# Sparse attention and two expert layers on one core: zero rows beside the last keys, and a new way through the fourth step

## The chip, the cores and the metric

The kernel runs on one core of one Trainium2 chip. The metric is the device time of one execution in microseconds, as a median over runs. TensorE does the matmuls, VectorE (DVE) and ScalarE (ACT) the element-wise work, GpSimd (POOL) part of it, and SyncE (SP) issues the DMAs.

## The reference

The reference chains three layers. Attention has 2 batches, 8 heads, 576 tokens and a head size of 64; each row of scores keeps its 32 largest entries. Its output, 1152 x 512, goes through four experts (512 to 1024 to 512, ReLU), weighted by shares per token, and then through a gated layer (512 to 1536 to 512).

```python
scores = scale * np.matmul(q, k.transpose(0, 1, 3, 2))
kth = np.partition(scores, -top_k, axis=-1)[..., -top_k:-top_k + 1]
scores = np.where(scores >= kth, scores, -1000000000.0)
scores = scores - np.max(scores, axis=-1, keepdims=True)
attn = np.exp(scores)
attn = attn / (np.sum(attn, axis=-1, keepdims=True) + 1e-09)
x = np.matmul(attn, v)                       # then 1152 x 512
for e in range(E):
    out += p[:, e:e + 1] * (np.maximum(x @ w1[e], 0.0) @ w2[e])
return ((out @ w_a) * (out @ w_b)) @ w_out
```

## The kernel before

The 1152 tokens are nine tiles of 128 rows: four per batch for its first 512 tokens, and one mixed tile (MIX) with the last 64 tokens of both batches. The tiles are split into groups of 1, 2, 3 and 3 (SIZES). Attention runs in 36 steps, numbered n, from 0: for each group, for each of four pairs of heads, for each tile of the group. Steps 0 to 3 are the first group, 4 to 11 the second, 12 to 23 the third, 24 to 35 the fourth; the four mixed steps lie in the last.

A step does the same for both heads of the pair, called x. TensorE makes 128 x 576 scores (`scores`), and ScalarE copies them into a score place (`ss`, four places). `masked` finds the 32 largest on VectorE: four times MAX8 (line 603) with three MATCH_REPLACE8 between them (609), into a weight place (`es`, six places). Then GpSimd multiplies the largest and the 32nd value by constants (649), ScalarE makes Relu with a very steep slope, zero for what is kept (656), GpSimd subtracts it (659), ScalarE takes exp with the sum beside it (666), GpSimd adds 1e-9 (675), VectorE takes the reciprocal (676), and ScalarE scales (679). In step 3, called URGENT, each head goes through this chain alone, and the difference and the addition stand on VectorE (659, 673). `weigh` turns the weights on TensorE, copies them out of PSUM (706, 710) into one of three places `pt`, and multiplies them with v: four blocks of 128 keys and one of the last 64 (`vrem`), for each head in one half of TensorE's columns. At the end of a pair its result goes into `xf` (738, first group) or `xs` (744, 746, the others), as the input of the experts.

The first group's experts (`plain`) work in plain float32; the others (`experts`) and the gated layer split each value into a high and a low part. A weight unit of 512 KB lands in one of three places `raw`, or, for every fourth unit of `plain`, in `pw`; for `experts` ScalarE (767) and GpSimd or VectorE (768) split it.

The order of the work is not that of the code. Each piece is an Op with an engine, an estimated hold, a lag until others see it, a due time (`key`) and its inputs and buffers; `Plan.order` walks through the estimated time and always takes the ready piece with the smallest key. What comes out is a fixed list for each engine, and each engine works through its own in order: an instruction whose input isn't there holds all those behind it. Keys of attention are near n; those of expert matmuls begin at 1000 and of weight loads at 500, so that they fill what attention leaves.

Of the kernel before, what the change touches and what calls it, by code (L numbers as in the profile page):

```python
# [16 lines left out]
TOPK = 32  # L17
# [220 lines left out]
PAIRED, URGENT = (), 3  # L238


def body(tc, q, k, v, probs, w1, w2, wa, wb, wo, out):
# [42 lines left out]
    ident = const("ident", [128, 128])  # L284
    identr = const("identr", [128, 128], F32R)
    pr = const("pr", [128, NT, E])
# [5 lines left out]
    vrem = [const(f"vrem{b}", [REM, H, D]) for b in range(B)]  # L292
# [91 lines left out]
    def consts():  # L384
        make_identity(nc, ident)
        nc.vector.tensor_copy(identr, ident)
        nc.gpsimd.memset(qm.bitcast(F32), 0.0)
        nc.gpsimd.memset(facs[:, :, 0], -scale)
        nc.gpsimd.memset(facs[:, :, 1], STEEP)

    ready = gpsimd(1900, consts, -1e6, (), ())

    loads = []
    for i, t in enumerate(TILES):
        for rows_, view in token_rows(t, probs):
            loads.append(load(lambda i=i, rows_=rows_: pr[rows_, i], lambda view=view: view, 2.0, nbytes=4096))
# [7 lines left out]
    shared = vector(900, shares, 3.5, loads, ())  # L404
# [13 lines left out]
    def keys(b, h2, key, eng):  # L418
# [27 lines left out]
        for j in range(2):  # L446
# [8 lines left out]
            o = tensor(5 * TURN_R, turn, key + 0.02, sp[j] + krem_done[b][h + j] + [ready], [at, st_])  # L455
# [21 lines left out]
    def start_pair(c, h2, n):  # L477
# [65 lines left out]
        for b in batches(tiles):  # L543
            vt = vts.tile(n)
            pair.v[b] = vt
            pair.vd[b] = [load(
                lambda vt=vt: vt.ap.rearrange("p (h m d) -> p h m d", h=2, m=M4), lambda b=b: main_rows(v, b, h), n - 2.5, (), [vt]
            )]
            if b not in vrem_done:
                vrem_done[b] = load(lambda b=b: vrem[b], lambda b=b: last_rows(v, b), n - 2.4, (), (), 131072)  # L550
        return pair

    def scores(pair, j, i, n):
# [24 lines left out]
        o = tensor(4 * len(bs) * mm_r(HALF), emit, n - AHEAD, after, [at] + used)  # L578
# [8 lines left out]
    def masked(sd, n):  # L587

        m8, ends, sums = m8s.tile(), endss.tile(), sumss.tile()
        W = TOPK + 17 if n in PAIRED else TOPK  # L590
        m8v = lambda: m8.ap[:, 0:2 * W].rearrange("p (x n) -> p x n", x=2)
# [3 lines left out]
        last = []  # L595

        def top(x, src, c0, rounds, width, key, done):

            for r in range(rounds):
# [5 lines left out]
                )  # L605
                if r < rounds - 1:
# [9 lines left out]
        for x in range(2):  # L616
            s = sd[x][0]
            key = n + (0.4 if urgent else 0.001) * x
            if n not in PAIRED:
                last.append(top(x, [lambda s=s: s.ap, lambda x=x: e[x].ap], 0, TOPK // 8, S, key, sd[x][1]))  # L620
                continue


            got = []
            for i, op in enumerate((ALU.max, ALU.min)):
                half = lambda x=x, i=i: e[x].ap[:, i * HALF:(i + 1) * HALF]
                po = gpsimd(
                    pool_(HALF), lambda s=s, half=half, op=op: nc.gpsimd.scalar_tensor_tensor(half(), s.ap[:, 0:HALF], 1.0, s.ap[:, HALF:S], op0=ALU.mult, op1=op),
                    n - 0.4 + 0.1 * i, [sd[x][1]], [s, e[x]],
                )  # L630
                got.append(top(x, [half, half], TOPK * i, TOPK // 8 // (i + 1), HALF, key + 0.005 * i, po))

            o = vector(
                85, lambda x=x: nc.vector.tensor_tensor(
                    m8v()[:, x, TOPK:TOPK + 16], m8v()[:, x, TOPK - 2:TOPK - 18:-1], m8v()[:, x, TOPK:TOPK + 16], op=ALU.min
                ), -600, got, [m8],
            )
            last.append(vector(
                85, lambda x=x: nc.vector.tensor_reduce(
                    out=m8v()[:, x, TOPK + 16:W], in_=m8v()[:, x, TOPK - 1:TOPK + 16], axis=mybir.AxisListType.X, op=ALU.max  # L640
                ), -600, [o], [m8],
            ))

        ks = -3000 if urgent else n + 0.1
        out_, ex = [], []
        for xs_ in ([0], [1]) if urgent else ([0, 1],):
            x0, x1 = xs_[0], xs_[-1] + 1
            en = gpsimd(
                150, lambda x0=x0, x1=x1: nc.gpsimd.tensor_tensor(endv()[:, x0:x1], m8v()[:, x0:x1, ::W - 1], facs[:, x0:x1], op=ALU.mult),  # L649
                -4000 if urgent else -500, [last[x] for x in xs_] + [ready], [m8, ends],  # L650
            )
            for x in xs_:
                s = sd[x][0]

                a = scalar(
                    S, lambda x=x, s=s: nc.scalar.activation(e[x].ap, s.ap, AF.Relu, bias=endv()[:, x, 1:2], scale=-STEEP),  # L656
                    ks, [en], [s, e[x], ends], sbuf=True, ptr=True,
                )
                sub = lambda eng, x=x, s=s: eng.tensor_tensor(e[x].ap, s.ap, e[x].ap, op=ALU.subtract)  # L659
                if urgent:  # L660
                    b = vector(dve(S), lambda sub=sub: sub(nc.vector), ks, [a], [s, e[x]], port=True)
                else:
                    b = gpsimd(pool_(S), lambda sub=sub: sub(nc.gpsimd), ks, [a], [s, e[x]])
                ex.append(scalar(
                    S,
                    lambda x=x: nc.scalar.activation(  # L666
                        e[x].ap, e[x].ap, AF.Exp, bias=endv()[:, x, 0:1], scale=scale, accum_out=sums.ap[:, x:x + 1]
                    ),
                    ks, [b], [e[x], ends, sums], sbuf=True, ptr=True, extra=92,
                ))  # L670
            sv = lambda x0=x0, x1=x1: sums.ap[:, x0:x1]
            if urgent:
                sm = vector(70, lambda sv=sv: nc.vector.tensor_scalar(sv(), sv(), 1e-9, None, op0=ALU.add), ks, ex[-1:], [sums])
            else:
                sm = gpsimd(290, lambda sv=sv: nc.gpsimd.tensor_scalar(sv(), sv(), 1e-9, None, op0=ALU.add), -500, ex, [sums])
            rc = vector(70, lambda sv=sv: nc.vector.reciprocal(sv(), sv()), ks if urgent else -500, [sm], [sums])  # L676
            for x in xs_:
                out_.append((e[x], scalar(
                    S, lambda x=x: nc.scalar.activation(e[x].ap, e[x].ap, AF.Copy, scale=sums.ap[:, x:x + 1]),  # L679
                    ks, [rc], [e[x], sums], sbuf=True, ptr=True,  # L680
                )))
# [4 lines left out]
    def weigh(pair, i, ed, n):  # L686
# [6 lines left out]
        for e, done in ed:  # L693
# [8 lines left out]
            o = tensor(4 * TURN_F + 40, turn, n + 0.5, [done, ready], [at, e])  # L702
# [16 lines left out]
        def emit():  # L719

            for r0, r1, b in groups:
                for m in range(M4 + 1):
                    for j in range(2):
                        vt = pair.v[b].ap.rearrange("p (h m d) -> p h m d", h=2, m=M4)
                        l, rows = (vt[:, j, m], 128) if m < M4 else (vrem[b][:, pair.h + j], REM)
                        mm(
                            ov()[j * D:(j + 1) * D, i, r0:r1], l, pt[j].ap[0:rows, m * 128 + r0:m * 128 + r1],
# [4 lines left out]
            1150, emit, n + 0.6, ptd + sum((pair.vd[b] for b in bs), []) + [vrem_done[b] for b in bs], [pair.o] + pt + [pair.v[b] for b in bs]  # L732
# [44 lines left out]
    def plain_unit(src, a):  # L777
        s = nxt()
        plains[0] += 1
        r = (wraws if plains[0] % 4 else pws).tile()  # L780
# [301 lines left out]
```

## Time and profile before

| | us |
|---|---|
| median of 3 runs | 867.97 (867.55 to 869.35) |
| the profiled execution | 866.53 |
| its span, first to last instruction | 864.7 |
| TensorE busy | 826.5 |
| VectorE busy | 715.8 |
| ScalarE busy | 544.6 |
| GpSimd busy | 265.2 |

The mean granted TensorE clock was 0.998. Busy time of TensorE includes overlapping matmuls, so the start of one group of records and that of the next tell more about a group's price than its own length does. Idle time behind an engine's name in square brackets is what it stood still ahead of an instruction, with what released it.

### The profile page before, as it was taken

To read this page: it belongs to the slowest core of one execution; us is meant where nothing else is said; L and a number is where in the kernel's file an instruction comes from. 1 tells how busy PE (TensorE), PEld (TensorE's weight loads), DVE (VectorE), ACT (ScalarE), POOL (GpSimd) and SP (SyncE) were. 2 spreads that over 40 slices of the span, in tenths; PEclk is the share of its full clock that TensorE was granted. 3 is DMA by queue.
4 is the path that set the end of the run, shared out by engine and by line. 5 is a ranking of instruction groups with operands and counts; after the bars stand their busy time and mean duration, and the time that the engine had idled before them with its cause. 6 is when DMAs were issued, how large, how long until landed. Compare 5 with 4: busy or idle time off the path is not lost. (4 is left out here: it accounts for less than half of the span.)

```text
span 864.7 us, 14129 instructions
## 1 busy us (share of the span) xinstructions
PE 826.5 (96%) x5168; PEld 728.0 (84%) x5168; DVE 715.8 (83%) x1381; ACT 544.6 (63%) x1042; POOL 265.2 (31%) x245
## 2 busy tenths in 40 slices
PE   5579999999999999999999999999999999999997
PEld 4466777788888888889888888889999989999996
DVE  6899999999999999999978999555434888999723
ACT  5888987899989998877765655333324535344310
POOL 2634442887897965853320000000000000000000
PEclk9999999999999999999999999999999999999999
DMA  7727977844564444342234556434101313323003
GB/s 197 244 90 257 297 239 235 268 149 145 168 185 150 152 148 153 98 123 97 75 122 156 179 177 195 122 122 128 44 1 49 98 49 98 91 81 98 25 1 109
DMA packets 83509, 117.06 MB, mean 135 GB/s; under 512 B 10608, under 2 KB 54640, under 8 KB 83440
## 3 DMA queue, kind: packets, MB, share of 16 engines
q1 hardware_dynamic: 83440, 116.17, 42.9%
q8 instruction: 40, 0.66, 0.3%
q14 instruction: 29, 0.24, 0.1%
HBM read 109.07 MB, written 7.08 MB: 134 GB/s over the span
## 5 line engine op out<-in xcount | busy, mean ns | idle before, releaser
L603 DVE MAX8 low<-low 128x8 f32<-128x576 f32 x288 | 203.7, 747 | 3.4 <-ACT low L582 3.3
L362 PE MATMUL ps<-xs,mid 128*128 128x384 f32 (+1 forms) x1152 | 205.1, 322 | 1.3 <-POOL mid L768 1.0
L362 PE MATMUL ps<-mid 128*128 128x512 f32 x768 | 198.6, 396 | 2.1 <-DVE mid L841 2.0
L362 PEld LDWEIGHTS ps<-xs,mid 128*128 128x128 f32 x1152 | 184.4, 189 | 11.5 <-issue 2.5
L362 PEld LDWEIGHTS ps<-mid 128*128 128x128 f32 x768 | 139.2, 188 | 28.5 <-DVE mid L841 6.0
L609 DVE MATCH_REPLACE8 low<-low 128x576 f32<-128x576 f32 x216 | 159.3, 743 | 0.0
L362 PE MATMUL ps<-xs,big 128*128 128x384 f32 x864 | 152.8, 335 | 0.0
L362 PEld LDWEIGHTS ps<-xs,big 128*128 128x128 f32 x864 | 149.9, 188 | 1.6 <-DVE low L1033 0.3
L767 ACT ACTIVATE mid<-raw 128x1024 fp32r<-128x1024 f32 x96 | 101.5, 1059 | 66.3 <-issue 39.9
L768 POOL TENSOR_TENSOR mid<-raw,mid 128x1024 fp32r<-128x1024 f32 x48 | 115.2, 2408 | 11.9 <-ACT mid L767 8.9
L659 POOL TENSOR_TENSOR low<-low 128x576 f32<-128x576 f32 x70 | 98.9, 1428 | 32.8 <-ACT low L656 31.0
L362 PE MATMUL ps<-big,mid 128*128 128x512 f32 x324 | 75.1, 390 | 0.0
L768 DVE TENSOR_TENSOR mid<-raw,mid 128x1024 fp32r<-128x1024 f32 x48 | 58.5, 1220 | 18.9 <-ACT mid L767 18.7
L362 PEld LDWEIGHTS ps<-big,mid 128*128 128x128 f32 x324 | 60.7, 188 | 12.3
L837 ACT ACTIVATE mid<-ps 128x384 fp32r<-128x384 f32 (+1 forms) x96 | 42.7, 450 | 33.0 <-PE ps L362 28.3
L859 DVE SCALAR_TENSOR_TENSOR ys<-ps,pr,ys 128x512 f32<-128x512 f32 x56 | 41.5, 747 | 24.3 <-PE ps L362 23.7
L841 DVE SCALAR_TENSOR_TENSOR mid<-ps,mid 128x384 fp32r<-128x384 f32 (+1 forms) x96 | 48.0, 506 | 15.1 <-ACT mid L837 14.6
L656 ACT ACTIVATE low<-low 128x576 f32<-128x576 f32 x72 | 53.4, 772 | 7.6 <-POOL low L649 7.4
L1012 ACT ACTIVATE low<-ps 128x384 f32<-128x384 f32 x36 | 17.6, 489 | 64.1 <-PE ps L362 64.0
L365 PE MATMUL ps<-ident,low 128*128 128x128 f32 (+1 forms) x360 | 50.6, 282 | 7.3 <-ACT low L679 7.1
L679 ACT ACTIVATE low<-low 128x576 f32<-128x576 f32 x72 | 52.9, 776 | 6.1 <-DVE low L676 6.1
L666 ACT ACTIVATE low<-low 128x576 f32<-128x576 f32 x72 | 55.7, 774 | 0.7 <-POOL low L659 0.7
(76 smaller groups left out, 1040.0 us busy)
## 6 DMA issues: line engine op xcount, KB each, us to landing
raw<-in_moe_w_dram SPq DMA_DIRECT2D x120, 512.0 KB, 3.7
big<-kscr SPq DMA_DIRECT2D x20, 576.0 KB, 4.8
low<-in_v_dram SPq DMA_DIRECT2D x24, 256.0 KB, 4.1
low<-in_moe_w_a_dram SPq DMA_DIRECT2D x12, 512.0 KB, 3.8
low<-in_moe_w_b_dram SPq DMA_DIRECT2D x12, 512.0 KB, 3.8
low<-in_moe_w_out_dram SPq DMA_DIRECT2D x12, 512.0 KB, 3.6
kscr<-big SPq DMA_DIRECT2D x8, 576.0 KB, 4.4
ys<-in_moe_w_dram SPq DMA_DIRECT2D x8, 512.0 KB, 4.6
```

Source lines behind the costliest of these rows:

```text
L362: nc.tensor.matmul(out, l, r, **kw)
L365: nc.tensor.transpose(out, a, i)
L603: 62 + 1.04 * width, lambda at=at, cs=cs: nc.vector.max(m8v()[:, x, cs], at()), key + 0.02 * r, [done],
L609: lambda at=at, cs=cs: nc.vector.match_replace(out=src[1](), in_to_replace=m8v()[:, x, cs], in_values=at(), imm_value=LOW),
L656: S, lambda x=x, s=s: nc.scalar.activation(e[x].ap, s.ap, AF.Relu, bias=endv()[:, x, 1:2], scale=-STEEP),
L659: sub = lambda eng, x=x, s=s: eng.tensor_tensor(e[x].ap, s.ap, e[x].ap, op=ALU.subtract)
L666: lambda x=x: nc.scalar.activation(e[x].ap, e[x].ap, AF.Exp, bias=endv()[:, x, 0:1], scale=scale, accum_out=sums.ap[:, x:x + 1]),
L679: S, lambda x=x: nc.scalar.activation(e[x].ap, e[x].ap, AF.Copy, scale=sums.ap[:, x:x + 1]),
L767: hi = scalar(1024, lambda: nc.scalar.activation(u.ap[:, 0:1024], r.ap, AF.Copy), 500 + s, [ld], [u, r], sbuf=True)
L768: sub = lambda eng: eng.tensor_tensor(u.ap[:, 1024:2048], r.ap, u.ap[:, 0:1024], op=ALU.subtract)
L837: n, lambda h=h, p=p: nc.scalar.activation(h.ap[:, 0:n], p.ap[:, 0:n], AF.Relu), -1000, [o], [h, p]
L841: lambda h=h, p=p: nc.vector.scalar_tensor_tensor(h.ap[:, n:2 * n], p.ap[:, 0:n], 0.0, h.ap[:, 0:n], op0=ALU.max, op1=ALU.subtract),
```

## The change

- The last block of keys is multiplied over 128 rows: `vrem` and the last column block of each `pt` have zeros in rows 64 to 127, filled once by GpSimd (`zeros`, with a hold of 1500 and key 0.2). Each weighting waits for that.
- The identity for float32 turns is the same memory as the one for float32r, so 128 words are free. It is made in `xf` first.
- `raw` has four places instead of three; the attention region is 500 words smaller, all that was unused. In `plain` every fifth unit goes to `pw`.
- The lag of the GpSimd addition ahead of the reciprocal gets 1200 ns more (SLACK). That moves later in VectorE's list what the list supposes to be ready later.
- Step 3 goes through a new function `hurried`. When the first MAX8 of a head is there, GpSimd makes the bias from the largest value and ScalarE takes exp of all 576 scores into another weight place, beside the rest of the top-32. When the 32nd value is there, VectorE multiplies with (score >= 32nd) and sums, adds 1e-9, takes the reciprocal and multiplies.
- Estimates are changed: a turn of keys 640 instead of 440, scores 30 more, a turn of weights 40 more, a weighting 1245 instead of 1150. The ten loads of the shares have key 4.0 instead of 2.0, and the shares themselves 5.2 instead of 3.5.
- The branch for half-width top-32 (PAIRED, empty) is taken out. `experts` takes a unit from `ahead` where one is there; nothing puts one there.

```diff
-PAIRED, URGENT = (), 3
+SLACK = 1200
+URGENT = 3
...
-    ident = const("ident", [128, 128])
     identr = const("identr", [128, 128], F32R)
+    ident = identr.bitcast(F32)
...
-    vrem = [const(f"vrem{b}", [REM, H, D]) for b in range(B)]
+    vrem = [const(f"vrem{b}", [128, H, D]) for b in range(B)]
...
-    raw = Region("raw", 3 * 1024, F32)
-    wraws = raw.slots("wraw", 3, 1024)
-    low = Region("low", 12800, F32)
+    raw = Region("raw", 4 * 1024, F32)
+    wraws = raw.slots("wraw", 4, 1024)
+    low = Region("low", 12300, F32)
...
-        make_identity(nc, ident)
-        nc.vector.tensor_copy(identr, ident)
+        make_identity(nc, xf[:, 0])
+        nc.vector.tensor_copy(identr, xf[:, 0])
...
+    def zeros():
+        for b in range(B):
+            nc.gpsimd.memset(vrem[b][REM:128], 0.0)
+        for p in pts.aps:
+            nc.gpsimd.memset(p[REM:128, MAIN:MAIN + 128], 0.0)
+    zeroed = gpsimd(1500, zeros, 0.2, [ready], ())
...
-            loads.append(load(lambda i=i, rows_=rows_: pr[rows_, i], lambda view=view: view, 2.0, nbytes=4096))
+            loads.append(load(lambda i=i, rows_=rows_: pr[rows_, i], lambda view=view: view, 4.0, nbytes=4096))
...
-    shared = vector(900, shares, 3.5, loads, ())
+    shared = vector(900, shares, 5.2, loads, ())
...
-            o = tensor(5 * TURN_R, turn, key + 0.02, sp[j] + krem_done[b][h + j] + [ready], [at, st_])
+            o = tensor(640, turn, key + 0.02, sp[j] + krem_done[b][h + j] + [ready], [at, st_])
...
-        o = tensor(4 * len(bs) * mm_r(HALF), emit, n - AHEAD, after, [at] + used)
+        o = tensor(4 * len(bs) * mm_r(HALF) + 30, emit, n - AHEAD, after, [at] + used)
...
+                if r == 0:
+                    firsts.append(done)
...
+        if urgent:
+            return hurried(sd, n, m8v, m8, ends, endv, sums, firsts, last)
...
+        sm.lag += SLACK
+        rc = vector(70, lambda: nc.vector.reciprocal(sums.ap, sums.ap), -500, [sm], [sums])
...
+    def hurried(sd, n, m8v, m8, ends, endv, sums, firsts, last):
+        out_ = []
+        for x in range(2):
+            s, e = sd[x][0], es.tile(n)
+            en = gpsimd(
+                150, lambda x=x: nc.gpsimd.tensor_tensor(endv()[:, x, 0:1], m8v()[:, x, 0:1], facs[:, x, 0:1], op=ALU.mult),
+                -4000, [firsts[x], ready], [m8, ends],
+            )
+            ex = scalar(
+                S, lambda x=x, s=s, e=e: nc.scalar.activation(e.ap, s.ap, AF.Exp, bias=endv()[:, x, 0:1], scale=scale),
+                n + 0.1, [en], [s, e, ends], sbuf=True, ptr=True,
+            )
+            sv = lambda x=x: sums.ap[:, x:x + 1]
+            def mask(x=x, s=s, e=e, sv=sv):
+                nc.vector.scalar_tensor_tensor(
+                    e.ap, s.ap, m8v()[:, x, TOPK - 1:TOPK], e.ap, op0=ALU.is_ge, op1=ALU.mult, accum_out=sv()
+                )
+                nc.vector.tensor_scalar(sv(), sv(), 1e-9, None, op0=ALU.add)
+                nc.vector.reciprocal(sv(), sv())
+                nc.vector.tensor_scalar(e.ap, e.ap, sv(), None, op0=ALU.mult)
+            out_.append((e, vector(1450, mask, -3000, [ex, last[x]], [s, e, m8, sums], port=True)))
+        return out_
...
-            o = tensor(4 * TURN_F + 40, turn, n + 0.5, [done, ready], [at, e])
+            o = tensor(4 * TURN_F + 80, turn, n + 0.5, [done, ready], [at, e])
...
-                        l, rows = (vt[:, j, m], 128) if m < M4 else (vrem[b][:, pair.h + j], REM)
+                        l = vt[:, j, m] if m < M4 else vrem[b][:, pair.h + j]
                         mm(
-                            ov()[j * D:(j + 1) * D, i, r0:r1], l, pt[j].ap[0:rows, m * 128 + r0:m * 128 + r1],
+                            ov()[j * D:(j + 1) * D, i, r0:r1], l, pt[j].ap[:, m * 128 + r0:m * 128 + r1],
                             start=(m == 0), stop=(m == M4),
                         )
...
-            1150, emit, n + 0.6, ptd + sum((pair.vd[b] for b in bs), []) + [vrem_done[b] for b in bs], [pair.o] + pt + [pair.v[b] for b in bs]
+            1245, emit, n + 0.6, [zeroed] + ptd + sum((pair.vd[b] for b in bs), []) + [vrem_done[b] for b in bs], [pair.o] + pt + [pair.v[b] for b in bs]
...
-        r = (wraws if plains[0] % 4 else pws).tile()
+        r = (wraws if plains[0] % 5 else pws).tile()
...
-    ydone = {}
+    ydone, ahead = {}, {}
...
-                    unit = w_unit(w1[e, :, u:u + 256].rearrange("(a p) n -> p a n", p=128), KD, late)
+                    unit = ahead.pop(u) if u in ahead else w_unit(w1[e, :, u:u + 256].rearrange("(a p) n -> p a n", p=128), KD, late)
```

## Rows read from the trace of the kernel before

**Rows 1.** The page, busy us (share of the span) and instructions of each engine.
```profile
PE 826.5 (96%) x5168; PEld 728.0 (84%) x5168; DVE 715.8 (83%) x1381; ACT 544.6 (63%) x1042; POOL 265.2 (31%) x245
```
**Rows 2.** Stretches: length, busy us of PE, PEld, DVE, ACT, POOL, PE clock, DMA share, GB/s.
```profile
9.45:53.22 43.77, 28.48 (x173) 23.65 (x172) 39.26 (x83) 34.60 (x75) 21.45 (x28) 0.96 0.64 189
53.22:66.34 13.12, 10.25 (x91) 7.72 (x89) 13.02 (x33) 10.63 (x26) 3.14 (x5) 1.00 0.42 134
66.34:153.20 86.86, 84.74 (x632) 65.70 (x633) 82.91 (x179) 72.19 (x146) 35.05 (x42) 1.00 0.80 258
153.20:305.30 152.10, 148.66 (x1118) 129.41 (x1118) 148.92 (x324) 137.55 (x271) 128.83 (x95) 1.00 0.55 171
305.30:457.90 152.60, 150.96 (x1086) 133.61 (x1084) 138.82 (x275) 119.91 (x241) 75.07 (x68) 1.00 0.37 118
457.90:860.20 402.30, 398.76 (x2057) 363.89 (x2055) 289.25 (x486) 164.11 (x274) 0.00 (x0) 1.00 0.31 95
```
**Rows 3.** Timelines of DVE and PE (start, length, what): the third group's handover.
```profile
304.78 0.56 DVE L746 TENSOR_TENSOR xs<-ps,xs 128x384 fp32r<-128x384 f32 x1
...
306.52 0.69 PE L362 MATMUL ps<-xs,mid 128*128 128x384 f32 x3
```
**Rows 4.** Timeline of PE: a plain weighting with what follows, then part of a mixed one.
```profile
201.71 1.09 PE L362 MATMUL ps<-low 128*64 128x128 f32 x16
202.73 0.44 PE L362 MATMUL ps<-low,vrem 64*64 64x128 f32 x4
203.10 0.80 PE L362 MATMUL ps<-big 128*128 128x288 f32 x4
...
333.64 0.69 PE L362 MATMUL ps<-low 128*64 128x64 f32 x16
334.25 0.33 PE L362 MATMUL ps<-low,vrem 64*64 64x64 f32 x4
334.52 0.69 PE L362 MATMUL ps<-low 128*64 128x64 f32 x16
```
**Rows 5.** Groups of PE by shape: count, busy us and mean ns, idle before.
```profile
L362 PE MATMUL ps<-low,vrem 64*64 64x128 f32 x128 | 13.9, 294 | 0.0
...
L362 PE MATMUL ps<-low,vrem 64*64 64x64 f32 x32 | 2.7, 242 | 0.0
```
**Rows 6.** Timeline of DVE: the reciprocals of steps 0 to 2.
```profile
29.98 0.17 DVE L676 RECIPROCAL low<-low 128x2 f32<-128x2 f32 x1 [2.90 <-POOL low L675]
...
42.31 0.17 DVE L676 RECIPROCAL low<-low 128x2 f32<-128x2 f32 x1 [0.86 <-POOL low L675]
...
50.37 0.17 DVE L676 RECIPROCAL low<-low 128x2 f32<-128x2 f32 x1 [0.36 <-POOL low L675]
```
**Rows 7.** Timelines of DVE, ACT and PE: the end of step 3.
```profile
51.89 1.41 DVE L603 MAX8 low<-low 128x8 f32<-128x576 f32 x2
...
54.67 1.41 DVE L659 TENSOR_TENSOR low<-low 128x576 f32<-128x576 f32 x2
...
58.85 1.44 ACT L679 ACTIVATE low<-low 128x576 f32<-128x576 f32 x2
...
66.01 0.28 ACT L738 ACTIVATE xf<-ps 128x128 f32<-128x128 f32 x1 [1.82 <-PE ps L362]
...
62.90 1.67 PE L362 MATMUL ps<-big 128*128 128x288 f32 x8
```
**Rows 8.** Groups of DVE by shape: a product with one operand in the gated layer.
```profile
L971 DVE TENSOR_SCALAR low<-low 128x512 f32<-128x512 f32 x36 | 15.2, 422 | 10.3 <-ACT low L970 10.3
```
**Rows 9.** Timeline of POOL: a fill at the start, a difference of step 2.
```profile
1.23 0.95 POOL L387 MEMSET qm<- 128x1024 f32 x1
...
44.88 1.42 POOL L659 TENSOR_TENSOR low<-low 128x576 f32<-128x576 f32 x1 [0.89 <-ACT low L656]
```
**Rows 10.** Timeline of DVE: the copy of the identity and what follows.
```profile
1.32 1.01 DVE L386 CAST identr<-ident 128x128 fp32r<-128x128 f32 x1 [1.32 <-POOL ident masks.py:199]
3.99 1.36 DVE L411 TENSOR_TENSOR big<-low,big 128x256 fp32r<-128x256 f32 x5 [1.66 <-ACT big L409]
```

More of the change, by code (lines that the diff above doesn't have):

```diff
@@ L549, in start_pair @@
             if b not in vrem_done:
-                vrem_done[b] = load(lambda b=b: vrem[b], lambda b=b: last_rows(v, b), n - 2.4, (), (), 131072)
+                vrem_done[b] = load(lambda b=b: vrem[b][0:REM], lambda b=b: last_rows(v, b), n - 2.4, (), (), 131072)
         return pair
@@ L594, in masked @@
         e = [es.tile(n) for _ in range(2)]
-        last = []
+        last, firsts = [], []
         def top(x, src, c0, rounds, width, key, done):
@@ L618, in masked @@
             key = n + (0.4 if urgent else 0.001) * x
[L619 to L629, printed above, removed]
-                )
-                got.append(top(x, [half, half], TOPK * i, TOPK // 8 // (i + 1), HALF, key + 0.005 * i, po))
@@ L633, in masked @@
[L633 to L681, printed above, removed]
@@ new lines, in masked @@
+            last.append(top(x, [lambda s=s: s.ap, lambda x=x: e[x].ap], 0, TOPK // 8, S, key, sd[x][1]))
+        if urgent:
+            return hurried(sd, n, m8v, m8, ends, endv, sums, firsts, last)
+        ks = n + 0.1
+        out_, ex = [], []
+        en = gpsimd(
+            150, lambda: nc.gpsimd.tensor_tensor(endv(), m8v()[:, :, ::TOPK - 1], facs, op=ALU.mult), -500, last + [ready], [m8, ends]
+        )
+        for x in range(2):
+            s = sd[x][0]
+            a = scalar(
+                S, lambda x=x, s=s: nc.scalar.activation(e[x].ap, s.ap, AF.Relu, bias=endv()[:, x, 1:2], scale=-STEEP),
+                ks, [en], [s, e[x], ends], sbuf=True, ptr=True,
+            )
+            b = gpsimd(
+                pool_(S), lambda x=x, s=s: nc.gpsimd.tensor_tensor(e[x].ap, s.ap, e[x].ap, op=ALU.subtract), ks, [a], [s, e[x]]
+            )
+            ex.append(scalar(
+                S,
+                lambda x=x: nc.scalar.activation(
+                    e[x].ap, e[x].ap, AF.Exp, bias=endv()[:, x, 0:1], scale=scale, accum_out=sums.ap[:, x:x + 1]
+                ),
+                ks, [b], [e[x], ends, sums], sbuf=True, ptr=True, extra=92,
+            ))
@@ new lines, in masked @@
+        sm = gpsimd(290, lambda: nc.gpsimd.tensor_scalar(sums.ap, sums.ap, 1e-9, None, op0=ALU.add), -500, ex, [sums])
+        sm.lag += SLACK
+        rc = vector(70, lambda: nc.vector.reciprocal(sums.ap, sums.ap), -500, [sm], [sums])
+        for x in range(2):
+            out_.append((e[x], scalar(
+                S, lambda x=x: nc.scalar.activation(e[x].ap, e[x].ap, AF.Copy, scale=sums.ap[:, x:x + 1]),
+                ks, [rc], [e[x], sums], sbuf=True, ptr=True,
+            )))
+        return out_
```

14 lines of the change are left out of this document (9 added, 5 removed).

## The prediction

> **What bounds the kernel now.** I read the busy shares first, then the engines stretch by stretch, then single waits. TensorE is busy 826.5 of 864.7 us [rows 1], so the first idea is that only its own work counts. The stretches show otherwise [rows 2]. From 9.45 to 66.34 us TensorE is busy 38.7 of 56.9 us, while VectorE is busy 39.26 of 43.77 and then 13.02 of 13.12: here the top-32 loops of steps 0 to 3 set the pace, and each us that VectorE stands still delays the first expert stage. From 66.34 on TensorE has 2.12 + 3.44 + 1.64 + 3.54 = 10.7 us idle in 794 us and sets the end. But up to 305.30 VectorE is nearly full too (82.91 of 86.86, 148.92 of 152.10): it is a second bound there, and after 305.30 it is not.
>
> How far apart the two are shows where the third group is handed over to the experts: VectorE writes the last part of the third group's input at 304.78 to 305.34, and TensorE takes it at 306.52 [rows 3]. So TensorE has 1.2 us in hand there. A gain of TensorE alone ahead of 305 is worth that much and what other work it can pull forward; the rest has to come from VectorE.
>
> **The change, part by part.**
>
> *Zero rows.* A plain step's weighting has 16 records of 128 rows in 1.02 us and 4 of 64 rows in 0.37 us [rows 4]. Records come in pairs, one for each half of the columns. With s for a pair and E for what each change of the array's shape adds, 8s + E = 1.02 and 2s + E = 0.37, so s = 0.108 and E = 0.154 us. In a step that mixes both batches 8s + E = 0.61 and 2s + E = 0.27 [rows 4]: s = 0.057, E = 0.156, and there are four such blocks. With 128 rows throughout a plain step has one block instead of two (one E less), a mixed step one instead of four (0.47 less). The 64-row records number 128 and 32 [rows 5]: 32 plain and 4 mixed steps. Four plain steps lie ahead of 66.34, where TensorE waits anyway: nothing. 20 lie between 66.34 and 305.30: 3.1 us. The last 8 plain and the 4 mixed: 1.23 + 1.87 = 3.1 us. Sum 6.2 us, at the least 5 (if the longer block has a slower end than its pieces). The added rows cost no time of their own: a matmul's price here goes by its columns, and these stay.
>
> *Later reciprocals.* Three reciprocals stand at the head of VectorE's queue until GpSimd has the sums: 2.90, 0.86 and 0.36 us, with the next top-32 instructions queued behind them [rows 6]. Sum 4.12. The added 1.2 us moves each later in the list. That removes the two small ones and 1.2 of the large one: 2.4. All of it, 4.1, if the longer times given to turns and scores also bring the list nearer to the chip. I take 3.0. Who waits for a later reciprocal: the two scalings on ScalarE and the turn; in these stretches they have other work. At the handover at 305 it is 1.2 us later, and takes the 1.2 us in hand away.
>
> *The fourth step.* Before, its top-32 ends at 53.30 and the second scaled weights at 58.85 + 1.44 = 60.29: 7.0 us through GpSimd, ScalarE, VectorE, ScalarE, VectorE, ScalarE [rows 7]. After, exp runs beside the top-32, and two masks follow on VectorE. One is a product over 576 columns (half of 1.41, 0.70), an add and a reciprocal on one column (0.15 each, a little under the 0.17 of the reciprocals in [rows 6]), and a multiplication by a column, 0.42 for 512 [rows 8], so 0.47 for 576: about 1.5. Two: 3.1, so the weights come 3.9 us earlier (3.3 if the last multiplication takes 0.75, as the other forms over 576 do). If exp came late, the masks would stand on VectorE with step 4's top-32 behind them. I cost this at nothing: exp's bias is ready after the first of four rounds, three rounds ahead of the mask. From the weights to the input of the first stage it is 66.01 - 60.29 = 5.7 us [rows 7]; taken as before. The window gets 6.9 us shorter in all, and the fill in it (the scores of a later step, 1.67 us at 62.90 [rows 7]) can slip behind it: I count three quarters, 1.2. TensorE's gain at 66: 3.0 + 3.9 - 1.2 = 5.7 us.
>
> For VectorE the masks are dearer than what they replace: 3.1 against two differences, 1.41 [rows 7], and four instructions on one column, 1.6 in all with overlap. It gains 3.0 - 1.5 = 1.5 us, and I add 1.0 of its 7.1 us idle between 66.34 and 305.30: 2.5 us.
>
> *Loads and zeros.* The ten small loads of the shares move behind later loads on SP's queue, and the shares themselves behind step 4 on VectorE; their reader, the first expert result, comes only after the first stage has begun: nothing either way, and four short VectorE instructions leave the stretch that counts. The zero fill is 2 x 512 and 3 x 128 columns on GpSimd, by 0.95 us for 1024 [rows 9] some 1.4 us, behind the constants and ahead of its other work. It could hold VectorE's copy of the identity, which took 1.01 us for 128 columns beside that fill [rows 10] where 512 take 0.42 [rows 8]; VectorE's next work is at 3.99 [rows 10], so 0 to 1.4 us; I take 0, since the copy ended with the first fill, 2.33 against 2.18.
>
> *Fourth weight place.* It lets one more unit of 512 KB load ahead. Attention loads go first by their due times. Against it stands at most one such transfer in front of a q or k load, 2.8 us at the 189 GB/s of 9.45 to 53.22 [rows 2]; for it, some of TensorE's waits behind 66. I take nothing (-1 to +2.8). The units taken from `ahead` are never put there in this diff: no effect. Nor have the shared identity and the removed half-width branch, which no step used.
>
> *New list.* Every engine's order is made anew. Today's waits on TensorE from 66.34 on, 10.7 us, can shrink or grow; I take no change, bounds -4 and +4.
>
> *A rule of the skill against it.* The Trainium skill, SBUF — State Buffer, section "SBUF: two separate sides", says that VectorE in its two-port modes and GpSimd lock one pair of ports for a whole instruction, and the later one stands still. The slow copy of [rows 10] agrees. By it the masks' last multiplication can be held by a GpSimd instruction under way, and the time would be that of the third rival, 862.9 instead of 860.0.
>
> **Sum.** Up to 305 TensorE could be 5.7 + 3.1 = 8.8 us earlier, VectorE allows 2.5 + 1.2 - 1.2 = 2.5, and TensorE can go on for a while on what needs only three quarters of the input: three PSUM places times three parts of 0.52 us (0.69 less its end [rows 3]) is 4.7, of which I count half, 2.3, as weights and results need places too. So 4.8 us there, and 3.1 behind it: 7.9. The profiled execution took 866.53 us, 1.83 outside its span. 866.53 - 7.9 = 858.6; the median of the runs stands 1.44 above that execution: 860.0 us.
>
> **The rivals.**
> 1. *VectorE gives nothing.* The recovered stalls come back as waits for scores, since four score places must be freed by GpSimd and ScalarE first. For it: ScalarE is busy 34.60 of 43.77 us there [rows 2]. Against: VectorE hardly waits for scores today. Then its account is -1.5 + 2.3 = 0.8, with 3.1: 866.53 - 3.9 + 1.44 = 864.0. Chance 0.15.
> 2. *TensorE alone sets the pace*: it finds enough other work at the handover. 866.53 - 11.9 + 1.44 = 856.1, and lower if the list also closes waits. Against it speaks VectorE's 97.9% [rows 2]. Chance 0.20.
> 3. *GpSimd holds the masks*, each for one difference of 1.42 us [rows 9]: 2.8 us less on VectorE, 862.9. Against: GpSimd is busy 3.14 of 13.12 us there [rows 2]. Chance 0.05.
> 4. *The switches stay*: E belongs to something else than the change of shape. The gain behind 305 is gone: 863.2. Against it: both kinds of steps give the same E. Chance 0.06.
> 5. *Slower.* The new list puts instructions at the head of TensorE's queue whose inputs aren't there, between 66 and 860. Price: today's 10.7 us twice over, 866.53 - 7.9 + 10.7 + 1.44 = 870.8. It decides once it loses more than 7.9 us. For it: nothing but that VectorE, ScalarE and GpSimd are all over 84% busy from 153 to 305 [rows 2], so a misjudged wait spreads. Against: the times given to turns, scores and weighting come nearer to the rows. Chance 0.07.
>
> **How the numbers follow.** The forecast has 0.47, its own range 856 to 863. For the range I reach from rival 2 with 3 us from the list (853) to behind rival 1 (866), which leaves rival 5 and some tails out. 0.2%, 1.7 us, is about what a measurement of this kernel can tell from no change. Faster by more: all but rival 5 and the tail of rival 1, 0.86. Within: 0.07. Slower: 0.07.
>
> **What would show it.** Right: no TensorE record of 64 rows in the weighting, and 20 records in 1.23 us; VectorE's waits at the reciprocal under 1.5 us ahead of 60; the first stage's input complete at 59 to 60 instead of 66.0; masks of about 1.5 us; the third group's input at 300 to 303, and TensorE with a few us more idle around it. Wrong: a mask with a wait in front of it; the handover at 305 unmoved, or TensorE far ahead of it without a wait; more than 15 us of waits behind 66.

## The result, and the profile after

| | before | after |
|---|---|---|
| median, us | 867.96 (867.55 to 869.35) | 854.03 (853.69 to 856.42) |
| profiled execution, us | 866.53 | 856.42 |
| its span, us | 864.7 | 854.6 |

The ratio is 0.9843, with a 95% interval of 0.9822 to 0.9864: 13.9 us faster, where 7.9 us were forecast. The two profiled executions are only 10.1 us apart: that of before lies 1.4 us under its median, that of after 2.4 us over. Every reading of the traces below is of those two.

The busy shares after [rows 1], and the stretches of before laid over the new trace [rows 2]:

```profile
PE 821.2 (96%) x5168; PEld 728.5 (85%) x5168; DVE 715.8 (84%) x1385; ACT 540.3 (63%) x1036; POOL 266.1 (31%) x250
```
```profile
9.45:53.22 43.77, 28.81 (x174) 22.95 (x174) 41.75 (x92) 36.56 (x79) 21.72 (x29) 0.98 0.63 200
53.22:66.34 13.12, 10.88 (x98) 9.31 (x98) 13.12 (x28) 8.13 (x18) 4.31 (x5) 0.94 0.50 164
66.34:153.20 86.86, 85.31 (x638) 66.47 (x639) 84.24 (x185) 71.81 (x148) 35.11 (x41) 1.00 0.80 260
153.20:305.30 152.10, 150.59 (x1145) 133.91 (x1140) 149.61 (x324) 138.30 (x276) 132.56 (x98) 0.99 0.55 178
```

TensorE's busy time falls by 5.3 us (826.5 to 821.2), and from 66 to 305 us it is idle 3.1 us instead of 5.6, from 66 to 500 us 5.4 instead of 8.9. VectorE stands still less ahead of 53 us (busy 41.75 against 39.26 of 43.77).

The work after the third group's results are turned is the same in both, so a few marks tell where the time went. All are starts of instructions in the traces: the copy of the first stage's last input (ACT, `xf`), and the last turn of each group's results (PE, `ps` from `ys`).

| us | first stage's input | first group turned | second | third | span |
|---|---|---|---|---|---|
| before | 66.0 | 170.1 | 313.9 | 500.7 | 864.7 |
| after | 63.8 | 165.0 | 306.5 | 490.6 | 854.6 |
| gained so far | 2.2 | 5.1 | 7.4 | 10.1 | 10.1 |

So only 2.2 us are gained by the start itself; the rest comes little by little up to 490 us. From there to the end both take 364.0 us.

These terms add up nearly to the gain: 2.2 us from the start, 3.5 us less idle time of TensorE from 66 to 500 us, and the 6.2 us that the prediction worked out for the zero rows behind 66, less 1.5 us that TensorE lost at its lower clock from 167 to 171 us (the rows stand below, with the run that has less work on VectorE) make 10.4, against 10.1. That says where the time went, not which edit sent it there; the experiments are about that.

The weighting of a plain step after, on the timeline of PE [rows 4]:

```profile
200.04 1.09 PE L364 MATMUL ps<-low 128*64 128x128 f32 x16
200.97 0.39 PE L364 MATMUL ps<-low,vrem 128*64 128x128 f32 x4
201.29 0.80 PE L364 MATMUL ps<-big 128*128 128x288 f32 x4
```

From its first record to the next group it takes 1.25 us, against 1.39. 1.23 was worked out.

The first steps on the timeline of DVE: the three reciprocals that had waits of 2.90, 0.86 and 0.36 us [rows 6], and the masks of the fourth step.

```profile
28.54 0.17 DVE L660 RECIPROCAL low<-low 128x2 f32<-128x2 f32 x1 [0.61 <-POOL low L657]
...
39.21 0.17 DVE L660 RECIPROCAL low<-low 128x2 f32<-128x2 f32 x1 [0.88 <-POOL low L657]
...
49.59 0.15 DVE L660 RECIPROCAL low<-low 128x2 f32<-128x2 f32 x1
49.66 0.74 DVE L613 MAX8 low<-low 128x8 f32<-128x576 f32 x1
50.32 0.80 DVE L684 SCALAR_TENSOR_TENSOR low<-low 128x576 f32<-128x576 f32 x1
51.04 0.08 DVE L684 DVE_READ_ACCUMULATOR low<-low 128x1 f32 x1
...
51.55 0.52 DVE L689 TENSOR_SCALAR low<-low 128x576 f32<-128x576 f32 x1
...
53.22 0.52 DVE L689 TENSOR_SCALAR low<-low 128x576 f32<-128x576 f32 x1
```

Waits of 4.12 us have become 1.49. The top-32 ends at 50.40 instead of 53.30, no mask has a wait in front of it, and the second scaled weights are there at 53.74 instead of 60.29. And yet the input of the first stage is complete only 2.2 us earlier. TensorE's timeline behind 53.74, with ScalarE's copy at its end, shows why [rows 7]:

```profile
54.33 1.33 PE L364 MATMUL ps<-low 128*64 128x128 f32 x16
55.49 0.38 PE L364 MATMUL ps<-low,vrem 128*64 128x128 f32 x4
55.81 1.36 PE L367 MATMUL ps<-identr,big 128*128 128x128 f32 x10
57.10 1.16 PE L364 MATMUL ps<-xf,raw 128*128 128x128 f32 x8
58.01 0.88 PE L367 MATMUL ps<-identr,big 128*128 128x128 f32 x8
59.24 1.31 PE L367 MATMUL ps<-identr,low 128*128 128x128 f32 x10 [0.35 <-ACT big L545]
61.75 0.76 PE L364 MATMUL ps<-big 128*128 128x288 f32 x4 [1.20 <-DMA big<-kscr]
62.44 1.09 PE L364 MATMUL ps<-low 128*64 128x128 f32 x16
```
```profile
63.83 0.28 ACT L748 ACTIVATE xf<-ps 128x128 f32<-128x128 f32 x1 [2.27 <-PE ps L364]
```

The weights wait from 53.74 to 59.24 behind the third step's weighting, eighteen turns of keys and q of later steps and a part of the first stage; then scores wait 1.20 us for a load of keys, and only behind them comes the weighting. From scaled weights to the input it is 10.1 us instead of 5.7.

The handover of the third group [rows 3], on the timelines of DVE and PE:

```profile
303.44 0.54 DVE L756 TENSOR_TENSOR xs<-ps,xs 128x384 fp32r<-128x384 f32 x1
```
```profile
295.58 3.33 PE L364 MATMUL ps<-xs,mid 128*128 128x384 f32 x18
...
304.36 0.77 PE L364 MATMUL ps<-xs,mid 128*128 128x384 f32 x3
```

VectorE completes the group's input 1.3 us earlier than before. TensorE takes the last quarter 0.4 us behind that, but has done 18 records of the first three quarters 9 us ahead of it; in the old order none came ahead.

### The profile page after: what moved, and what is told of

Its sections match the earlier page's. It is cut to its first block, busy times and chain, and to the rows that moved or that the text cites. A ratio compares the mean times of both kernels' runs of the same rounds, so it can differ in the third digit from the quotient of the medians.

```text
span 854.6 us, 14156 instructions
## 1 busy us (share of the span) xinstructions
PE 821.2 (96%) x5168; PEld 728.5 (85%) x5168; DVE 715.8 (84%) x1385; ACT 540.3 (63%) x1036; POOL 266.1 (31%) x250
## 5 line engine op out<-in xcount | busy, mean ns | idle before, releaser
L663 ACT ACTIVATE low<-low 128x576 f32<-128x576 f32 x70 | 51.0, 774 | 13.2 <-DVE low L660 13.2
L852 DVE SCALAR_TENSOR_TENSOR mid<-ps,mid 128x384 fp32r<-128x384 f32 (+1 forms) x96 | 48.2, 506 | 12.2 <-ACT mid L848 11.7
L593 ACT ACTIVATE low<-ps 128x576 f32<-128x576 f32 x72 | 46.8, 650 | 17.2 <-POOL low L648 11.8
L644 ACT ACTIVATE low<-low 128x576 f32<-128x576 f32 x70 | 53.1, 776 | 5.3 <-POOL low L638 5.2
L652 ACT ACTIVATE low<-low 128x576 f32<-128x576 f32 x70 | 54.4, 778 | 0.2
```

Of the source, the lines that this page charges most:

```text
L593: S, lambda: nc.scalar.activation(s.ap.rearrange("p (c n) -> p c n", c=2), at.ap[:, :, 0:HALF], AF.Copy),
L652: lambda x=x: nc.scalar.activation(e[x].ap, e[x].ap, AF.Exp, bias=endv()[:, x, 0:1], scale=scale, accum_out=sums.ap[:, x:x + 1]),
L852: lambda h=h, p=p: nc.vector.scalar_tensor_tensor(h.ap[:, n:2 * n], p.ap[:, 0:n], 0.0, h.ap[:, 0:n], op0=ALU.max, op1=ALU.subtract),
```

## The experiments

Every kernel was timed in turns with the kernel before on the same chip; its median there was 868.1, 867.8 and 867.5 us in the three sessions. The changed kernel was timed only for the result above, so a difference from its 854.03 us is one between sessions, in which the kernel before moved by 0.7 us. An edit that touches an estimate, a due time or a number of instructions changes every engine's list. Where the lists stay the same, that is said.

**Zero rows, undone in the new lists and made alone in the old ones.** The first kernel is the changed one with

```diff
-                        l = vt[:, j, m] if m < M4 else vrem[b][:, pair.h + j]
+                        l, rows = (vt[:, j, m], 128) if m < M4 else (vrem[b][0:REM, pair.h + j], REM)
-                            ... l, pt[j].ap[:, m * 128 + r0:m * 128 + r1],
+                            ... l, pt[j].ap[0:rows, m * 128 + r0:m * 128 + r1],
```

> The changed kernel with one thing undone: the last block of keys is multiplied over 64 rows again. All five engines' lists stay the same, so the new order keeps its worth and only the array's shape changes back. Theory A (each change of shape costs TensorE 0.15 us where it sets the end): 28 plain steps at 0.154 and 4 mixed ones at 0.467, so 854.0 + 6.2 = about 860, at least 859. Rival B (the switches were hidden, the new order made the gain): 856 at most. In the trace, A: the weighting of a plain step takes 1.39 us from its first record to the next group, and TensorE's waits behind 66 us stay as they are.

Measured: 859.93 us (0.9906 of before, 0.9891 to 0.9921), 5.9 over the changed kernel. On TensorE's timeline the step is back:

```profile
62.80 1.09 PE L364 MATMUL ps<-low 128*64 128x128 f32 x16
63.83 0.43 PE L364 MATMUL ps<-low,vrem 64*64 64x128 f32 x4
64.19 0.80 PE L364 MATMUL ps<-big 128*128 128x288 f32 x4
```

1.39 us again. Theory A holds: of the 13.9 us, 5.9 are changes of the array's shape (5.5 by the two ratios to the kernel before).

The other way round, the kernel before with the fill, `vrem` of 128 rows and the longer block, with its old lists:

> The kernel before with the zero rows alone: the fill stands with the constants, the last block is multiplied over 128 rows, and every engine's list is that of before. Theory A (each change of shape costs 0.15 us of TensorE wherever TensorE sets the end, whatever the list): 868 - 6 = 862, with at least 861 and at most 863. Rival B (up to 305 us VectorE sets the pace of the old list, so only the steps behind it pay): 865, 3 us less than before.

Measured: 864.23 us (0.9956, 0.9942 to 0.9970): 3.5 us faster, between the two theories. The marks seem to speak for rival B: its second group is turned at 313.9 as before, its third at 497.8 instead of 500.7. Of the 3.1 us ahead of 305 nothing is left there, and the 3.1 behind it come in nearly whole. On DVE's and PE's timelines the handover stands where it stood [rows 3]:

```profile
304.81 0.55 DVE L750 TENSOR_TENSOR xs<-ps,xs 128x384 fp32r<-128x384 f32 x1
```
```profile
306.50 0.69 PE L362 MATMUL ps<-xs,mid 128*128 128x384 f32 x3
```

But the gain isn't lost at that point. The first stage's input comes at 66.85, 0.8 later than before, behind the longer fill and a stretch from 24.0 to 37.6 us in which TensorE's granted clock was 0.50 (1.00 there in the kernel before). At 170 the run is 0.1 ahead, so 1.0 us of TensorE's gain has come through. Then the clock falls again, to 0.50 from 170.8 to 174.2 (1.00 in the kernel before). PE's timeline there, first of the kernel before, then of this run:

```profile
170.27 2.98 PE L362 MATMUL ps<-xs,mid 128*128 128x256 f32 x21
```
```profile
170.14 4.35 PE L362 MATMUL ps<-xs,mid 128*128 128x256 f32 x21
```

The same 21 records take 1.4 us longer, and from there to 314 the run makes up 1.2 us once more. So ahead of 305 TensorE gained 2.2 of the 3.1 us, and the late start and the fall took as much away; that the handover comes at the same time is, by these numbers, a coincidence of this execution. It shows no gain that is lost at the handover, and rival B isn't borne out. What the clock did in the executions that weren't profiled is known only as a mean (0.987 to 0.995 in the six), so how far it explains the 3.5 us of the median stays open.

**Is it VectorE's load that sets the handover?** The changed kernel without the third MATCH_REPLACE8 in steps 4 to 23, TensorE's list unchanged:

```diff
-                        lambda at=at, cs=cs: nc.vector.match_replace(
+                        (lambda: None) if r == 2 and 4 <= n <= 23 else lambda at=at, cs=cs: nc.vector.match_replace(
```

> The changed kernel without the third MATCH_REPLACE8 of both heads in steps 4 to 23, so those steps keep the 24 largest entries and repeat the last eight; the lists are the same otherwise. It takes 40 x 0.72 = 29 us of VectorE out of the stretch from 64 to 301 us. Theory A (VectorE is a second bound up to the third group's handover): the handover comes over 5 us earlier, and the time falls to 851 or below. Rival B (TensorE alone sets the pace there): the handover comes earlier, but the time stays within 853 to 855.

Measured: 854.96 us (0.9852, 0.9835 to 0.9868), no faster than the changed kernel. The stretch from 66 to 300 us, first of the changed kernel, then of this one, and the handover in this one:

```profile
66.00:300.00 234.00, 230.88 (x1726) 195.75 (x1726) 228.95 (x498) 206.13 (x412) 164.45 (x137) 0.99 0.64 207
```
```profile
66.00:300.00 234.00, 230.11 (x1734) 195.39 (x1734) 203.00 (x422) 207.31 (x415) 165.56 (x137) 1.00 0.66 208
```
```profile
302.33 0.54 DVE L756 TENSOR_TENSOR xs<-ps,xs 128x384 fp32r<-128x384 f32 x1
```

VectorE is busy 203.0 instead of 229.0 us, and the handover comes 1.1 us earlier instead of over 5. Even this 1.1 us isn't VectorE's. In the profiled execution of the changed kernel TensorE's granted clock was 0.57 from 167 to 171 us, in this one 1.00, and the same 24 records, on PE's timelines, took 4.63 and 3.14 us:

```profile
166.65 4.63 PE L364 MATMUL ps<-xs,mid 128*128 128x256 f32 x24 [1.32 <-DVE mid L852]
```
```profile
167.07 3.14 PE L364 MATMUL ps<-xs,mid 128*128 128x256 f32 x24 [1.32 <-DVE mid L852]
```

Theory A has fallen for the new lists. VectorE was 98% busy without setting the pace: relieved of 26 us, it waits for other engines instead, longest for ScalarE (10.0 us at the inputs of the groups, `xs`, where the changed kernel has 1.1). Whether its load sets the pace in the old lists wasn't tried.

**The added lag at the reciprocals.** The changed kernel with `SLACK = 0`:

> The changed kernel without the added lag of 1200 ns ahead of the reciprocals. Theory A (waits at the head of VectorE's queue ahead of 50 us delay everything up to the third group's handover): waits at the reciprocals ahead of 50 us grow from 1.5 to 3 or 4 us, the fourth step's top-32 ends 2 us later, and the time is 855.5 to 857. Rival B (VectorE does not decide there, TensorE's own list does): 853 to 855, whatever the waits at the reciprocals are.

Measured: 857.45 us (0.9879, 0.9865 to 0.9894), 3.4 over the changed kernel and just above A's range. The waits at the three reciprocals are 2.69, 1.00 and 0 us, 2.2 more in all, as A says; the first stage's input comes at 64.7, 0.9 later. Whether the other 2.5 us have to do with the lag depends on what new lists do by themselves, which the next runs tell.

**New lists with the same instructions.** One number, once up and once down by 10 ns:

```diff
-            1245, emit, n + 0.6, [zeroed] + ptd + ...
+            1255, emit, n + 0.6, [zeroed] + ptd + ...
```

> The changed kernel with one estimate changed by 10 ns: a weighting is supposed to take 1255 instead of 1245. No instruction is added or taken away, but the lists of all engines come out differently. Theory A (the lists are as good as the estimates): 853 to 855. Rival B (where the list changes, single misjudged waits make some us either way): over 1.5 us away from 854.0. What comes out is the size below which a run with a new list says nothing about one part of the change.

> The changed kernel with the weighting supposed to take 1235 instead of 1245 ns: a third draw of its lists. Theory A (a draw moves the time by some 4 us, and 854.0 is at the good end): 855.5 to 860. Rival B (1255 was an outlier): 853 to 855.

Measured: with 1255 it is 857.81 us (0.9876, 0.9856 to 0.9897), with 1235 it is 865.72 (0.9978, 0.9965 to 0.9992), more than either theory had. With the same instructions and an estimate changed by under 1%, the time goes from 854.0 to 865.7 us; at 1235 nearly all of the gain is gone, though the zero rows are still there. The input of the first stage is hardly touched: 63.8, 64.6 and 64.9 us for 1245, 1255 and 1235. TensorE's waits between 66 and 500 us show a part of the difference, first after, then with 1235; the columns are who waited for whom, us in total, times, the longest:

```profile
PE ps L364 <- DVE mid L852: 2.5, 3, 1.3
PE ps L364 <- DMA raw<-in_moe_w_dram: 1.1, 1, 1.1
PE ps L367 <- DVE mid L852: 1.1, 2, 0.9
PE ps L364 <- ACT low L936: 1.0, 2, 0.7
```
```profile
PE ps L367 <- ACT low L663: 4.4, 3, 2.3
PE ps L367 <- DVE mid L852: 1.5, 3, 0.8
PE ps L364 <- ACT low L936: 1.1, 2, 0.7
```

The longest of the new waits, on the timelines of PE and ACT:

```profile
169.11 1.29 PE L367 MATMUL ps<-identr,low 128*128 128x128 f32 x5 [2.27 <-ACT low L663]
```
```profile
167.29 1.10 ACT L777 ACTIVATE mid<-raw 128x1024 fp32r<-128x1024 f32 x1
168.24 1.48 ACT L663 ACTIVATE low<-low 128x576 f32<-128x576 f32 x2
```

A turn of weights stands at the head of TensorE's list, while ScalarE has a weight unit's copy of 1.1 us ahead of the scaling it needs. All of TensorE's waits there come to 8.3 us, against 5.9. With 1.1 us at the input and 1.3 behind the third group's turn, where TensorE's granted clock was 0.50 from 500.3 to 503.7, that is 4.8 of the 9.1 us by which the two profiled executions differ; where the others lie isn't settled.

The kernel without the lag, with 1255 as well:

> The kernel of e2_no_slack (changed kernel, no added lag at the reciprocals) with the weighting supposed to take 1255 instead of 1245 ns. Theory A (the lag is worth 2 to 4 us): 860 to 862, that is 2 to 4 above the 857.8 of e8_hold_1255, which has the lag and the same estimate. Rival B (the 3.4 us of e2 were the draw): 858.5 or below, perhaps under e8.

Measured: 868.21 us (1.0006, 0.9992 to 1.0019), 10.4 over the run with the lag and 1255 and beyond both theories. Its input comes at 65.0. TensorE's clock can have a part in this: it was at 0.50 from 64.1 to 67.5 and from 306.4 to 313.2 us, where the profiled execution with the lag had 1.00. So both pairs are slower without the lag, by 3.4 and 10.4 us, while the start loses under 1 us. Against a spread of 11.7 us between draws two pairs aren't enough to give the lag a price: that stays open.

**The fourth step's old way.** The changed kernel with Relu, difference, exp, addition, reciprocal and scaling in step 3, as before, and everything else new:

```diff
-            return hurried(sd, n, m8v, m8, ends, endv, sums, firsts, last)
+            return urgent_(sd, n, m8v, m8, ends, endv, sums, last, e)
```

The function `urgent_` itself, left out here, holds the old chain.

> The changed kernel with the fourth step's old way: Relu, difference, exp, addition, reciprocal and scaling behind the top-32. Theory A (the time from top-32 to scaled weights passes to the end): the weights are ready 3 to 4 us later, and the time is 856 to 858. Rival B (the turn of these weights stands behind other turns in TensorE's list anyway, 5.6 us behind their being ready): the input of the first stage comes at 64 to 66 us, and the time stays within 853 to 855.

> The kernel of e3_old_fourth (changed kernel, fourth step's old way) with the weighting supposed to take 1255 instead of 1245 ns: the same instructions in another draw of the lists. Theory A (the old way puts step 3's Relu and exp between step 2's two scalings on ScalarE, so that the input of the first stage is late in any list): the input comes after 66 us, and the time is 862 or above. Rival B (most of the 13 us of e3 were the draw): 860 or below, the input by 66.

Measured: 867.03 us (0.9989, 0.9977 to 1.0000) with 1245 and 865.66 (0.9986, 0.9975 to 0.9996) with 1255. The first is far above what either theory of its run had, the second is where its theory A had it. In both draws the first stage's input comes late, at 70.2 and 70.3 us: 6.4 and 5.7 us later than in the kernels with the new way and the same estimate. The place where it begins is ScalarE. Its timeline in the first of the two kernels, then in the changed one:

```profile
50.48 0.78 ACT L663 ACTIVATE low<-low 128x576 f32<-128x576 f32 x1 [0.69 <-DVE low L660]
51.16 1.43 ACT L679 ACTIVATE low<-low 128x576 f32<-128x576 f32 x2
...
53.12 0.77 ACT L663 ACTIVATE low<-low 128x576 f32<-128x576 f32 x1
```
```profile
49.78 1.44 ACT L663 ACTIVATE low<-low 128x576 f32<-128x576 f32 x2
```

In these lists step 3's Relu (L679) stands between the two scalings of step 2 (L663), so step 2's weighting on TensorE is late, and step 3's stands behind it. The new way takes Relu and the scaling of step 3 off ScalarE. But the old way doesn't need this order. In the kernel before, which has the old way too, ScalarE makes both scalings of step 2 together, and the input comes at 66.0:

```profile
50.57 1.44 ACT L679 ACTIVATE low<-low 128x576 f32<-128x576 f32 x2 [0.53 <-DVE low L676]
```

So the 6.4 and 5.7 us are the price of the old way in two lists made with the new estimates, not in any list. TensorE's clock can have a share in them as well. In the middle of this it was at its lower level (0.50, third number from the end) for 10.2 and 13.6 us in these two runs, and in the changed kernel for some 3.4 (51.4 to 54.8):

```profile
53.70:63.90 10.20, 8.41 (x48) 6.99 (x48) 10.20 (x27) 6.54 (x14) 0.04 (x1) 0.50 0.12 35
```
```profile
50.80:64.40 13.60, 10.22 (x54) 8.34 (x55) 13.60 (x33) 9.77 (x20) 0.71 (x2) 0.50 0.24 73
```

How much of the delay is the clock wasn't told apart, and where the rest of the 13.0 and 7.9 us lies isn't settled.

**The fill ahead of the fourth step's turn.** Two due times by 0.5 later put the eighteen turns behind it:

```diff
-        key = n - OPERANDS
+        key = n - OPERANDS + (0.5 if n == 6 else 0.0)
...
-            keys(1, prep, n + 2.0, "POOL")
+            keys(1, prep, n + 2.0 + (0.5 if prep == 0 else 0.0), "POOL")
```

> The changed kernel with two due times moved by 0.5: the turns of the second batch's first keys and of the q of steps 6 and 7 stand behind the fourth step's turn and weighting in TensorE's list instead of ahead of them. Theory A (these 18 turns, 2.2 us, delay the first stage's input and with it the end): the input comes at 60 to 61.5 instead of 63.8 us, and the time is 851 to 852.5. Rival B (TensorE is full from 50 us on, so the turns only change places with the stage's start): the input comes as early, but the time is 853 to 855.

Measured: the input comes at 60.8 us, as expected, and the first group is turned at 160.8, 4.2 us ahead of the changed kernel. But the second is turned at 315.6, 9.1 behind it, the third at 494.8, 4.2 behind it, and the time is 861.09 us (0.9925, 0.9913 to 0.9938), 7.1 slower. Neither theory had that. TensorE's longest waits from 157 to 316 us were for the split of weight units on GpSimd, so I tried whether attention, now earlier, takes GpSimd from them:

> The kernel of e4_fill_behind with GpSimd's difference in steps 4 to 23 over 96 of 576 columns, and a flat slope in Relu there, so that the weights of those steps are not the reference's; the lists are the same. It takes 40 differences from 1.4 to some 0.4 us, 40 us of GpSimd. Theory A (in e4 attention comes earlier and takes GpSimd from the splitting of the expert weights, and TensorE waits for that): TensorE's waits for the split on GpSimd between 157 and 316 us fall from 4.0 to under 1 us, and the time from 861.1 to 857 or below. Rival B (e4's list is bad in other places): 860 or above.

Measured: 861.73 us (0.9929, 0.9914 to 0.9945). The wait of TensorE from 157 to 316 us, first of the kernel above, then of this one:

```profile
PE ps L364 <- POOL mid L778: 4.0, 3, 2.3
```
```profile
PE ps L364 <- POOL mid L778: 4.0, 4, 1.8
```

GpSimd is busy 109 instead of 132 of those 159 us, and the wait is the same: it isn't GpSimd's load. Theory A has fallen. That the places in the lists make the wait is argued, not shown. From 61 to 495 us all waits of TensorE come to 11.0 us in the kernel above, against 7.1 in the changed one; what else makes this draw slow isn't settled.

**Three weight places.** The changed kernel with three places in `raw` and every fourth unit of `plain` in `pw`:

> The changed kernel with three places for raw weights again, and every fourth unit of the plain stage in the other place. Theory A (TensorE waits for weights only where their split is late, not for the load): within the spread of the draws, 853 to 859, and no wait of TensorE for a weight load over 1.5 us in all. Rival B (the fourth place carries a good part of the gain): 861 or above, with waits for weights in the plain stage between 66 and 160 us.

Measured: 856.07 us (0.9862, 0.9849 to 0.9875), 2.0 over the changed kernel and inside the spread of draws. From 60 to 160 us no wait of TensorE is for a weight load. The fourth place carries no part that can be told.

None of the tried versions beats the changed kernel.

## Why the prediction was right or wrong

*Zero rows: right.* 6.2 us were worked out from four rows, 5.9 measured with the lists held fixed, and the block takes 1.25 us where 1.23 was expected. In the old lists the median gained only 3.5 us; the trace there shows 5.1 us gained from 66 us on and 2.2 lost to a late start and to the clock.

*Later reciprocals: right in the wait.* 3.0 of 4.12 us were to be recovered, 2.6 were. Without the lag the same waits come to 3.69. But "each us that VectorE stands still delays the first expert stage" failed: 2.2 us more of these waits moved that stage's input by 0.9. What the lag is worth at the end stays open (two pairs, 3.4 and 10.4 us).

*The fourth step: right up to the weights, wrong behind them.* Top-32 to weights is 3.3 us instead of 7.0, where 3.1 was expected; a mask takes 1.67 instead of 1.5 (a read of the accumulator, and 0.52 for the multiplication). The step that failed is "from the weights to the input of the first stage it is 5.7 us, taken as before". It was 10.1, since TensorE's list held other work in front; I let 1.2 us of that work slip behind, and all of it stayed ahead. The start gained 2.2 us instead of 5.7. One thing I had costed at nothing, that ScalarE is rid of Relu and scaling of the fourth step, mattered in the two lists that were tried with the old way.

*VectorE as a second bound: not borne out, and a cause of the low forecast.* The cap of 4.8 us at 305 came from VectorE's 97.9% and from the 1.2 us in hand. In the new lists 26 us less work on VectorE moved nothing: a busy share of 98% was no proof of a bound. TensorE began the group 9 us ahead of the handover, one of the signs that I had named for being wrong. I had counted half of what three PSUM places allow, 2.3 us, and it was 18 records in 3.2 us. TensorE was 7.4 us ahead at the second group's turn, and would have been 8.9 without the fall at 167, though VectorE's handover had moved by only 1.3 us. For the old lists no run shows the bound either. The second rival, TensorE alone, with 856.1 us, was the nearest.

*The new list: the term that was mis-sized.* I took no change, with bounds of 4 us either way. TensorE's idle time from 66 to 500 us fell from 8.9 to 5.4 us, inside that. But the same instructions with an estimate of 1235 instead of 1245 take 11.7 us more: the bounds should have been three times as wide. The changed kernel is a good draw, and only a part of the 13.9 us, the 5.9 of the zero rows and the earlier input, belongs to its edits by themselves. That the time came out so far below the forecast is luck in that sense: the three draws, 854.0, 857.8 and 865.7, have a mean of 859.2, near the 860.0 of the forecast, but not by its reasons, since the start gave less and VectorE held back less than it had. At a due time that brings the input 3 us forward the end was 7 us later.

*Fourth place, loads, zeros: nothing, as taken.* The copy of the identity takes 1.01 us again, beside a longer fill on GpSimd, and VectorE's next work starts at 3.95 instead of 3.99. The third rival's waits in front of the masks aren't there: after 50 us GpSimd has nothing to do until 57.8, so no run shows whether it would hold the masks.

## What to carry to other kernels

A change of the matmul's shape in the middle of a stream had a fixed price here, 0.154 us, which two blocks of different length give by two equations; zeros to fill the shape cost nothing, since the price went by columns. Where a fixed list per engine is made from estimates, test one part with the lists held fixed, or time several draws: here 10 ns in one estimate moved the end by up to 11.7 us, more than most edits. And test a suspected bound by taking load off it: an engine that is 98% busy may only be following another's order. And before two traces are set against each other mark by mark, look at the granted clock: here one fall moved all later marks by 1.4 to 1.5 us, as much as some of the effects that were sought.

## What the runs showed of the hardware

A change between 128 x 64 and 64 x 64 of the array cost 0.154 us of TensorE at float32, nearly as much as three pairs of records of 64 columns (0.057 each). The VectorE instruction that also sums had a read of the accumulator of 0.08 us behind it.

TensorE's granted clock fell in the middle of work in the profiled execution of the changed kernel, to 0.66 of full speed on average in this stretch:

```profile
50.00:55.00 5.00, 4.39 (x26) 3.92 (x28) 4.79 (x14) 3.93 (x8) 0.00 (x0) 0.66 0.12 26
```

Its levels are 2.4 and 1.2 GHz, so about two thirds of these 5 us ran at the lower one. There the 16 records of a weighting take 1.16 us to the next group (54.33 to 55.49) instead of 0.93 (200.04 to 200.97). TensorE had waited 2.49 us ahead of 50.60. Before had such a fall between 40 and 50 us (granted 0.83 there), beside a wait of 2.75 us ahead of 43.34.

The fall at 167 came behind a wait of 1.32 us ahead of 166.65 and cost 1.5 us. The run with less work on VectorE had the same wait ahead of the same records and no fall; the kernel before and that with zero rows alone had the same waits within 0.2 us ahead of 170, and only in the second did the clock fall. So the same list of TensorE's instructions gave an execution with such a fall and one without, and no run here shows what decides it.
